# Stating the order of TensorE, ScalarE and VectorE in the units of two expert layers

## The chip, the core and the metric

One core of one Trainium2 chip runs the whole program in one launch. The metric is device time in microseconds (us) of that core; of the kernel before three runs are shown, and one more execution was profiled. Engines are named as in the profile: TensorE (PE, with its weight loads as PEld), VectorE (DVE), ScalarE (ACT), GpSimd (POOL) and SyncE (SP), which issues the loads of weights.

## The reference

Attention with pooled queries feeds two layers of experts, each of which sends a token to one expert. Cut to what matters:

```python
attn_out = softmax(scale * pool2(q) @ k.T) @ v          # 4 batches, 8 heads -> x of 2304 rows, 512 wide
# layer 1: only rows with x @ w_skip > 0, the others pass through
e = argmax(xc @ w_gate); g = softmax(xc @ w_gate)[e]
x[do_compute] = xc + g * (relu(xc @ w1[e]) @ w2[e])
# layer 2: all rows, with its own gate and an output gate
e = argmax(x @ w_gate2); g = softmax(x @ w_gate2)[e]; o = sigmoid(x @ w_output_gate)[e]
out = g * o * (relu(x @ w1b[e]) @ w2b[e])               # 8 experts a layer, 512 -> 1024 -> 512
```

## The kernel before, in words

**Attention** fills the first 575 us and is not touched by the change. At its end each token has been put into a table of its layer and expert, and from there the work goes in **units**: a unit takes up to 128 or 256 rows of one expert through both products. `unit(m, kind, e, pos)` (L964) emits one, with m = 0 for layer 1 and m = 1 for layer 2:

- P: 256 rows of an expert that was chosen early; it starts a layer and is emitted in the same block as the first F.
- F: the first 128 rows of every expert (up to 128, possibly none). It always runs.
- D: 256 more rows, in an `If` per number of rows that there are.
- S: a last 128 rows, in another `If`.

The loop at L1100 to L1116 emits for every expert F, then `If(code > 0)` (L1108) with up to eight nested `If`s that hold a D each (L1109) and one that holds S (L1114). In this data layer 1 runs P, F0, F1, F2 with two D, F3, F4, F5 with S, F6, F7; layer 2 runs P, F0, F1 with D, F2 with D, F3, F4 with D, F5 with three D, F6, F7 with S, as the stretches of TensorE's instructions show.

**Rows.** `fetch` (L822) reads the unit's place in the table and issues two indirect DMAs on POOL, each gathering 128 rows into xg. `xprep` (L211) turns them: TensorE transposes 128 columns at a time into pX (L215), ScalarE copies pX to xh as fp32r (L218), and VectorE takes the rest, xl (L219). A unit prepares the rows of the *next* unit; it fetches them near its own start.

**First product of F and S.** `gemm1_S` (L829) has rows as weights: two halves f of 512 columns, each 12 matmuls (L842), hooks between them, and a copy by ScalarE of each finished half (L846, into ht and xc). Then both halves are transposed (L851), and `relu_split` (L222) makes h: one ScalarE operation in layer 1 (L224), ScalarE and VectorE in layer 2 (hh at L227, hl at L228). D and P have weights as weights (`gemm1_D`, L231 to L241).

**Second product.** `gemm2` (L854) accumulates a row block into pY, in two halves f: in layer 1 four fp32 matmuls each (L860), in layer 2 twelve of fp32r each (L866). `evac` (L870 to L874) writes pY into yo on VectorE and `scatter` (L876) sends yo by an indirect DMA. The last `evac` of a unit is emitted as the first thing of the next one, behind a tiny POOL copy of indices (idp, L973).

**Weights of the next expert.** Of an expert's 16 chunks `split` (L190) casts one to fp32r on ScalarE (L205) and subtracts on VectorE to get the low half (L207); for layer 2 chunks 5, 7, 9, 11, 13 and 15 are subtracted on POOL. In layer 1 only chunks 0 to 7 are split. `pre` (L1005) does it for a list of chunks, in F and P alone. `load_w` and `load_w2` issue the loads on SP.

**Routing for layer 2.** Units of layer 1 route the rows they have just made: `route2` (L892) in four steps. Step 0 transposes yo and copies it (L889, L890), step 1 is a small product and a copy (L900, L901), step 2 a product (L914) and a chain of VectorE steps with two exponentials on ScalarE between (L916 to L929), step 3 a few tiny products and a last chain of VectorE steps (L933 to L953). `record` (L954) then writes two table rows by indirect DMAs on POOL.

**What sets the order.** Each engine runs its instructions in the order of the compiled program. In the units a scheduler chooses that order: it may bring an instruction forward past others that are not ready, and it may draw work past an `If`. Only edges made by `behind` hold something back. `foretell` (L1085) emits a branch hint for all engines: it loads the number of units from `mt` (a register load, L1103), computes a condition and issues the hint (L1150 in the profile). In F it is called by `ahead`, emitted after `load_w`.

In F and S of layer 1 `xprep` is held behind the first half of the second product (`XA = (1, 0)`); in layer 2 it is not.

Of the kernel before, what the change touches and what calls it, by code (L numbers as in the profile page):

```python
# [25 lines left out]
F = 1024  # L26
P = 128
# [31 lines left out]
JD = 8  # L59
POOL_L2 = (5, 7, 9, 11, 13, 15)  # L60
PS = (0, 1, 2, 4)
HP = (((1, 0, 1), (2, 2, 3), (3, 4, 5), (4, 6, 7)),) * 2
HR = ((1, 2, 2),) * 2
XA = (1, 0)
PB = (14, 16)
DVE_F = ((), ())
R2D = (2, 4, 5)
# [47 lines left out]
def build(ctx, tc, kT, qT, vt, wg, wa1, wa2, cst, out):  # L115
# [66 lines left out]
    def behind(i, js):  # L182
        for j in js:
            if j.ins.engine == i.ins.engine:
                tc.add_manual_dep(i.ins, j.ins.name,
                                  mybir.DependencyInfo(mybir.DependencyClass.NoSync, mybir.DependencyReason.DATA),
                                  reason="issue order")
        return i
# [22 lines left out]
    def xprep(n=2, after=()):  # L211
        o = []
        for h in range(n):
            for k in range(4):
                behind(nc.tensor.transpose(pX[h][:, k * P:(k + 1) * P], xg[:, h, k * P:(k + 1) * P], ident), after)  # L215
            px = pX[h].rearrange("p (k c) -> p k c", c=P)
            hs_ = slice(h * P, (h + 1) * P)
            o.append(nc.scalar.copy(xh[:, :, hs_], px))  # L218
            o.append(nc.vector.tensor_tensor(xl[:, :, hs_], px, xh[:, :, hs_].bitcast(F32), ALU.subtract))  # L219
        return o  # L220
# [30 lines left out]
    with ExitStack() as es_:  # L251
# [47 lines left out]
        pre = ap.tile([P, 96], F32, name="pre")  # L299
# [555 lines left out]
    def gemm2(m, i, o, h, fs):  # L855
        hc = slice(h * P, (h + 1) * P)
        for f in fs:
            if m == 0:
                for k in range(4):
                    j = nc.tensor.matmul(pY[o], hr[f][:, k, hc], w2r[i][:, 4 * f + k, :],  # L860
                                         start=(f + k == 0), stop=(f * k == 3))
                continue
            n = 12 * f
            for a, w in ((hh[f], w2h[i]), (hh[f], w2l[i]), (hl[f], w2h[i])):
                for k in range(4):
                    j = nc.tensor.matmul(pY[o], a[:, k, hc], w[:, 4 * f + k, :], start=(n == 0), stop=(n == 23))  # L866
                    n += 1
        return j

    def evac(m, h, tok):  # L870
        wv = tok[:, h, 1:2].bitcast(F32)
        if m == 0:
            return nc.vector.scalar_tensor_tensor(yo[:, h, :], pY[h], wv, xc[:, h, :], ALU.mult, ALU.add)
        return nc.vector.tensor_scalar(yo[:, h, :], pY[h], wv, None, ALU.mult)  # L874

    def scatter(m, h, tok, after=()):  # L876
        nc.gpsimd.tensor_copy(ids[h].bitcast(F32), tok[:, h, 0:1].bitcast(F32))
        i = nc.gpsimd.indirect_dma_start(  # L878
            out=(xb if m == 0 else out)[:, :],
            out_offset=bass.IndirectOffsetOnAxis(ap=ids[h].bitcast(U32), axis=0), in_=yo[:, h, :], in_offset=None,  # L880
            bounds_check=N - 1, oob_is_err=False)
        behind(i, after)
        for q in scat2[m] + (gath if m == 0 else []):
            tc.declare_no_dep(i.ins, q.ins, reason="every token has a row of its own")
        scat2[m].append(i)
# [69 lines left out]
    def record(h, after=()):  # L955
        i = nc.gpsimd.indirect_dma_start(
            out=tab[:, :], out_offset=bass.IndirectOffsetOnAxis(ap=pid2[:, h:h + 1], axis=0), in_=rec2[:, h, :],
            in_offset=None, bounds_check=2 * PC * P - 1, oob_is_err=False)
        behind(i, after)
        for q in scat:  # L960
            tc.declare_no_dep(i.ins, q.ins, reason="every token has a row of its own")
        scat.append(i)

    def unit(m, kind, e, pos, urgent=(), ahead=None):  # L964
        s = 9 * m + 1 + e
        i = s % 2
        first = kind == "P" and m == 0
        small = kind in "FS"
        pm = 0 if kind == "P" else m
        cp_ = nc.gpsimd.tensor_copy  # L970
        urgent = list(urgent)
        if not first:
            cp_(idp.bitcast(F32), idc.bitcast(F32))  # L973
            urgent.append(evac(pm, 1, idp))
        src = ts0 if first else idn
        if small:
            cp_(idc[:, 1, :].bitcast(F32), src[:, 0, :].bitcast(F32))
            nc.gpsimd.memset(idc[:, 0, 0:1], 1 << 20)
        else:
            cp_(idc.bitcast(F32), src.bitcast(F32))  # L980

        def head():
            if m == 0:
                if small:
                    nc.scalar.copy(xc[:, 1, :], xg[:, 0, :])
                else:
                    nc.scalar.copy(xc, xg)
            log = pm == 0 and not first and not (kind == "F" and e == 0)
            if log:
                record(0)  # L990
            g = fetch(m, pos) if kind != "P" else ()
            if not first:
                scatter(pm, 1, idp, g)
            if log:
                record(1, g)

        def r2(step):
            if pm == 0 and not first:
                route2(step)

        def pre(*cs):
            if kind in "FP":
                for c in cs:
                    split(s + 1, c, DVE_F[m], urgent if e == 0 else ())

        def half():
            evac(m, 0, idc)
            scatter(m, 0, idc)

        if kind == "D":  # L1010
            steps = {0: head, R2D[0]: lambda: r2(0), R2D[1]: lambda: r2(1), R2D[2]: lambda: r2(2)}
            gemm1_D(m, i, lambda c: steps[c]() if c in steps else None)
            gemm2(m, i, 0, 0, (0, 1))
            half()
            r2(3)
            xprep()
            gemm2(m, i, 1, 1, (0,))
            if m == 0:
                turn(0)
            if ahead:  # L1020
                ahead()
            gemm2(m, i, 1, 1, (1,))
            return
        if kind == "P":

            def post(c):
                if c == 0 and not first:
                    head()
                for r in range(4):
                    if PS[r] == c:  # L1030
                        r2(r)
                if c == 7:
                    if m:
                        record(0)
                        record(1)
                    unit_list(m)
                    nc.gpsimd.dma_start(ts[:, :PC, :], tabv[:, PC * m:PC * (m + 1), :])
                    fetch(m, 80, 1)
                if not first:
                    pre(c)  # L1040
                else:
                    for d in range(8):
                        if NP0 + d * (8 - NP0) // 8 == c:
                            pre(d)

            if first:
                head()
                load_w2(1)
            gemm1_D(m, i, post, range(NP0 if first else 0, 8))
            pre(*range(8, PB[m]))  # L1050
            gemm2(m, i, 0, 0, (0, 1))
            half()
            pre(*range(PB[m], 16))
            load_w(s + 2)
            gemm2(m, i, 1, 1, (0,))
            if m == 0:
                turn(0)
            j = gemm2(m, i, 1, 1, (1,))
            return xprep(1, after=[j])
        def hook(n):  # L1060
            if n == 0:
                head()
                if kind == "F" and m == 0:
                    load_w2(s + 1)
            for c in HP[m]:
                if c[0] == n:
                    pre(*c[1:])
            for c in range(3):
                if HR[m][c] == n:
                    r2(c)  # L1070

        gemm1_S(m, i, hook)
        j = gemm2(m, i, 1, 0, (0,))
        r2(3)
        xprep(2, [j] if XA[m] else ())
        pre(*range(8, 16))
        if kind == "F":
            load_w(s + 2)
            ahead()
        gemm2(m, i, 1, 0, (1,))  # L1080

    scat2 = [[], []]
# [5 lines left out]
    for m in range(2):  # L1088
# [7 lines left out]
        for e in range(E):  # L1096

            def ahead():
                if e == 0:
                    if m == 0:  # L1100
                        r = nc.gpsimd.value_load(eP[0:1, 3:4], min_val=0, max_val=7 * SL)
                        nc.gpsimd.dma_start(ts[:, PC:, :], tabv[:, PC:, :][:, ds(r, 2), :])
                    codes.extend(nc.values_load(mt[m][0:1, c:c + 1], min_val=0, max_val=18) for c in range(E))  # L1103
                foretell(f"any{m}{e}", codes[e] > 0)
# [49 lines left out]
```

## Time and profile before

| what | us |
|---|---|
| three runs | 1168.31, 1170.78, 1175.32 (median 1170.78) |
| the profiled execution, its own time | 1175.5 |
| span in the profile | 1173.8 |
| PE / DVE / ACT / POOL busy | 1056.1 / 764.5 / 567.9 / 362.2 |

The profile covers one execution; times in its rows count from the first instruction. The groups of instructions name what is written and read (out<-in), how often, the busy time, the mean duration in ns, and after the bar the idle time of that engine just before them with what ended it. A timeline row gives the start, the duration and, in brackets, the idle time before it. PEclk is the share of full speed that TensorE's clock was granted; it has two levels, 1.2 and 2.4 GHz.

### The profile page before, as it was taken

How to read it: one execution, taken by the hardware profiler on the slowest of the kernel's cores; microseconds unless marked ns; L12 is line 12 of the kernel's file. 1: busy time of each engine (PE TensorE's matmuls, PEld its weight loads, DVE VectorE, ACT ScalarE, POOL GpSimd, SP SyncE). 2: the span in 40 equal slices, each digit the busy share in tenths (PEclk: the TensorE clock that was granted, in tenths of full speed). 3: DMA queues.
4: the chain of work that ended last, by engine and by line, in shares of the span. 5: the costliest groups of instructions: out<-in, count | busy, mean ns of one | idle time of the engine just before them, and what ended most of it. 6: DMA issues, size and time to landing. Idle time of an engine off the chain costs nothing. (4 is left out here: it accounts for less than half of the span.)

```text
span 1173.8 us, 19240 instructions
## 1 busy us (share of the span) xinstructions
PE 1056.1 (90%) x6400; PEld 762.3 (65%) x6400; DVE 764.5 (65%) x1423; ACT 567.9 (48%) x1395; POOL 362.2 (31%) x429
## 2 busy tenths in 40 slices
PE   4799998999989999899998999998869887899977
PEld 2566665666656666675755765565758676788865
DVE  6789998899899998976355224546664437262252
ACT  3566665566656666555355224545363435231141
POOL 6222222212242221210224123344563526151151
PEclk9799998999999999999999999999999898999989
DMA  9644442244444431137277205854574527251010
GB/s 230 160 115 114 107 111 62 71 112 101 112 102 112 106 93 37 40 96 240 65 241 255 92 28 193 256 166 156 178 233 134 172 65 254 67 190 36 30 40 18
DMA packets 72946, 146.47 MB, mean 125 GB/s; under 512 B 12652, under 2 KB 21612, under 8 KB 72738
## 3 DMA queue, kind: packets, MB, share of 16 engines
q1 hardware_dynamic: 63330, 127.65, 37.6%
q0 software_dynamic: 9408, 16.48, 4.6%
q8 instruction: 77, 1.26, 0.5%
q14 instruction: 131, 1.07, 0.3%
HBM read 138.18 MB, written 15.05 MB: 131 GB/s over the span
## 5 line engine op out<-in xcount | busy, mean ns | idle before, releaser
L409 ACT ACTIVATE PT<-pS 128x288 f32<-128x288 f32 x576 | 206.5, 409 | 148.4 <-PE pS L408 145.2
L382 DVE TENSOR_REDUCE mx<-pA 128x1 f32<-128x1152 f32 x144 | 194.9, 1356 | 32.5 <-PE pA L377 20.3
L405 PE MATMUL pS<-QQ,KK 128*128 128x288 f32 x576 | 185.6, 335 | 22.2 <-ACT PT L409 21.1
L416 PE MATMUL pO<-PT,V 128*64 128x288 f32 x1152 | 181.0, 425 | 0.0
L408 PE MATMUL pS<-QM,KB 73*128 73x288 f32 x576 | 167.2, 302 | 0.0
L405 PEld LDWEIGHTS pS<-QQ,KK 128*128 128x128 f32 x576 | 111.3, 193 | 74.8 <-ACT PT L409 31.7
L362 POOL TENSOR_TENSOR QM<-qs,QQ 64x576 fp32r<-64x576 f32 x32 | 48.3, 1512 | 320.5 <-ACT QQ L348 248.8
L408 PEld LDWEIGHTS pS<-QM,KB 73*128 73x128 f32 x576 | 112.2, 195 | 0.0
L377 PE MATMUL pA<-KK,QQ 128*128 128x384 f32 x384 | 94.5, 357 | 18.4 <-DVE KK L332 10.0
L416 PEld LDWEIGHTS pO<-PT,V 128*64 128x64 f32 x1152 | 72.6, 137 | 55.1 <-issue 26.6
L860 PE MATMUL pY<-w2r,hr 128*128 128x512 f32 x240 | 108.1, 596 | 0.4 <-issue 0.4
L205 ACT CAST w1h<-raw 128x512 fp32r<-128x512 f32 x141 | 78.9, 621 | 51.5 <-PEq L1114 27.0
L429 DVE TENSOR_TENSOR acc<-acc,PT 128x576 f32<-128x576 f32 x128 | 95.1, 762 | 4.4 <-ACT PT L409 3.4
L207 DVE TENSOR_TENSOR w1l<-raw,w1h 128x512 fp32r<-128x512 f32 x126 | 88.7, 743 | 12.3 <-ACT w1h L205 11.2
L218 ACT CAST xh<-pX 128x512 fp32r<-128x512 f32 x56 | 30.9, 589 | 128.5 <-PE pX L215 101.8
L237 PE MATMUL pH<-xh,w1h 128*128 128x256 f32 x312 | 90.8, 291 | 1.3 <-DVE hl L228 1.0
L237 PE MATMUL pH<-xl,w1h 128*128 128x256 f32 x312 | 88.8, 285 | 1.2 <-DVE xl L219 1.2
L237 PE MATMUL pH<-xh,w1l 128*128 128x256 f32 x312 | 88.4, 284 | 0.0
L842 PE MATMUL pH<-w1h,xh 128*128 128x512 f32 x144 | 62.1, 431 | 22.6 <-ACT w1h L205 13.9
L377 PEld LDWEIGHTS pA<-KK,QQ 128*128 128x128 f32 x384 | 67.3, 200 | 22.3 <-DVE mx L382 11.7
L228 DVE SCALAR_TENSOR_TENSOR hl<-pH,hh 128x256 fp32r<-128x256 f32 (+1 forms) x74 | 36.0, 486 | 61.3 <-ACT hh L227 58.5
L860 PEld LDWEIGHTS pY<-w2r,hr 128*128 128x128 f32 x240 | 43.5, 190 | 46.0 <-issue 42.5
(219 smaller groups left out, 1969.3 us busy)
## 6 DMA issues: line engine op xcount, KB each, us to landing
raw<-wa SPq DMA_DIRECT2D x216, 256.0 KB
rawQ<-qT SPq DMA_DIRECT2D x64, 288.0 KB
rawK<-kT SPq DMA_DIRECT2D x64, 288.0 KB
w2r<-wa SPq DMA_DIRECT2D x72, 256.0 KB
V<-vt SPq DMA_DIRECT2D x16, 576.0 KB
xb<-xr SPq DMA_DIRECT2D x14, 288.0 KB
xg<-xb,idn POOLq DMA_INDIRECT x54
xb<-xr POOLq DMA_DIRECT2D x2, 288.0 KB
```

The costliest lines, as they stand in the source:

```text
L205: behind(nc.scalar.copy(h, r), after)
L207: behind(eng.tensor_tensor(l, r, h.bitcast(F32), ALU.subtract), after)
L237: nc.tensor.matmul(o, w[:, k, cc], x[:, k, :], start=(n == 0), stop=(n == 11))
L377: nc.tensor.matmul(o, QQ[h][i][:, u * P:(u + 1) * P], KK[h][i][:, cc], start=True, stop=True)
L382: i = nc.vector.tensor_reduce(mx[p % 2 if p or t < 5 else 1][:, t:t + 1], pA[:, :, :384], AX.XY, ALU.max)
L405: m = nc.tensor.matmul(o, KK[h][i][:, k], QQ[h][i][:, c], start=True, stop=False)
L408: nc.tensor.matmul(o, KB[h][p % 2][:64 + NB, k], QM[h][i][:64 + NB, c], start=False, stop=True)
L409: exps.append(nc.scalar.activation(PT[(p * KT + j) % 4][h][:, c], o, AF.Exp, scale=0.0625))
L416: i = nc.tensor.matmul(pO[f][64 * h:64 * h + 64, :HQ], V[p % 3][:, j, h, :], PT[(p * KT + j) % 4][h][:, c], start=(j == 0), stop=(j == KT ...
L429: nc.vector.tensor_tensor(a, a, t, ALU.add)
L842: nc.tensor.matmul(pH[f], x[:, k, :P], w[:, k, fc], start=(n == 0), stop=(n == 11))
L860: j = nc.tensor.matmul(pY[o], hr[f][:, k, hc], w2r[i][:, 4 * f + k, :], start=(f + k == 0), stop=(f * k == 3))
```

## The change

Four things. (1) Units F, D and S are emitted inside a region in which TensorE, ScalarE and VectorE issue their instructions in the order of the source; POOL and SP stay the scheduler's, and so does P. (2) In F and S the order of the source itself changes: chunks 6 and 7 are split after both transposed halves instead of after the first product's second half, step 2 of `route2` comes one hook later, and `xprep` stands behind the first half of the second product in both layers, between chunks 8 to 11 and 12 to 15. (3) `ahead`, the hint, follows `xprep` in F; in D of layer 1 it goes before the transposes of `turn`. (4) On POOL the first `record` also goes behind the two gathers.

```diff
-HP = (((1, 0, 1), (2, 2, 3), (3, 4, 5), (4, 6, 7)),) * 2
-HR = ((1, 2, 2),) * 2
-XA = (1, 0)
+HP = ((1, 0, 1), (2, 2, 3), (3, 4, 5), (6, 6, 7))
+HR = (1, 2, 3)
...
-    def unit(m, kind, e, pos, urgent=(), ahead=None):
+    def unit(m, kind, *a):
+        if kind == "P":
+            return unit_(m, kind, *a)
+        ET = mybir.EngineType
+        with tc.manual_schedule(engines={ET.PE, ET.Activation, ET.DVE}):
+            return unit_(m, kind, *a)
+
+    def unit_(m, kind, e, pos, urgent=(), ahead=None):
...
-            if log:
-                record(0)
             g = fetch(m, pos) if kind != "P" else ()
             if not first:
                 scatter(pm, 1, idp, g)
             if log:
+                record(0, g)
                 record(1, g)
...
             gemm2(m, i, 1, 1, (0,))
+            if ahead:
+                ahead()
             if m == 0:
                 turn(0)
-            if ahead:
-                ahead()
             gemm2(m, i, 1, 1, (1,))
...
-            for c in HP[m]:
+            for c in HP:
                 if c[0] == n:
                     pre(*c[1:])
             for c in range(3):
-                if HR[m][c] == n:
+                if HR[c] == n:
                     r2(c)
 
         gemm1_S(m, i, hook)
-        j = gemm2(m, i, 1, 0, (0,))
+        gemm2(m, i, 1, 0, (0,))
         r2(3)
-        xprep(2, [j] if XA[m] else ())
-        pre(*range(8, 16))
+        pre(*range(8, 12))
+        xprep(2)
+        if kind == "F":
+            ahead()
+        pre(*range(12, 16))
         if kind == "F":
             load_w(s + 2)
-            ahead()
         gemm2(m, i, 1, 0, (1,))
```

## Rows read from the trace of the kernel before

**Rows 1.** Layers 1 and 2: PE, PEld, DVE, ACT, POOL busy (x), PEclk, DMA share, GB/s.

```profile
575.00:820.00 245.00, 230.40 (x1131) 146.12 (x1129) 115.05 (x406) 106.29 (x223) 88.08 (x125) 1.00 0.52 166
820.00:1174.00 354.00, 302.49 (x1658) 256.77 (x1657) 161.43 (x243) 125.98 (x255) 144.27 (x189) 0.95 0.37 119
```

**Rows 2.** Groups of PE instructions in layer 2 (820 to 1174 us).

```profile
L866 PE MATMUL pY<-w2h,hl 128*128 128x512 f32 x184 | 52.5, 408 | 8.7 <-DVE hl L228 8.7
...
L842 PE MATMUL pH<-w1h,xh 128*128 128x512 f32 x72 | 30.8, 428 | 15.6 <-ACT w1h L205 9.6 <-ACTq L1108 3.1 <-DVEq L1109 1.3
...
L215 PE MATMUL pX<-cs,xg 128*128 128x128 f32 x124 | 19.5, 291 | 14.9 <-DMA xg<-xb,idn 14.9
```

**Rows 3.** Groups of PE instructions in layer 1 (575 to 820 us).

```profile
L215 PE MATMUL pX<-cs,xg 128*128 128x128 f32 x92 | 12.4, 277 | 2.5 <-DMA xg<-xb,idn 2.5
L889 PE MATMUL pX<-cs,yo 128*128 128x128 f32 x56 | 8.9, 279 | 2.3 <-DVE yo L873 2.2
```

**Rows 4.** Timeline of PE in F1 of layer 2, from its transposes on.

```profile
875.47 0.60 PE L851 MATMUL pH<-cs,ht 128*128 128x128 f32 x4
880.70 0.80 PE L215 MATMUL pX<-cs,xg 128*128 128x128 f32 x4 [4.64 <-DMA xg<-xb,idn]
881.30 1.06 PE L851 MATMUL pH<-cs,xc 128*128 128x128 f32 x4
...
886.36 1.18 PE L866 MATMUL pY<-w2h,hh 128*128 128x512 f32 x4
...
888.30 0.86 PE L866 MATMUL pY<-w2h,hl 128*128 128x512 f32 x3
```

**Rows 5.** Timeline of DVE in F4 of layer 2.

```profile
984.53 7.33 DVE L207 TENSOR_TENSOR w2l<-raw,w2h 128x512 fp32r<-128x512 f32 x1 [0.35 <-DMA raw<-wa]
```

**Rows 6.** Timeline of POOL in the same unit.

```profile
985.11 2.53 POOL L207 TENSOR_TENSOR w1l<-raw,w1h 128x512 fp32r<-128x512 f32 x2
987.60 3.71 POOL L207 TENSOR_TENSOR w2l<-raw,w2h 128x512 fp32r<-128x512 f32 x3
```

**Rows 7.** The same columns in two stretches that follow an idle TensorE.

```profile
914.80:917.80 3.00, 2.96 (x8) 2.37 (x9) 0.00 (x0) 2.16 (x5) 0.00 (x0) 0.57 0.03 8
...
712.00:715.00 3.00, 2.79 (x14) 2.24 (x15) 2.10 (x5) 1.80 (x4) 1.68 (x6) 1.00 0.83 258
```

**Rows 8.** Timeline of PE: first matmul of F2 in layer 2, of F3 in layer 1.

```profile
914.85 0.47 PE L842 MATMUL pH<-w1h,xh 128*128 128x512 f32 x1 [2.02 <-ACT w1h L205]
...
712.21 0.49 PE L842 MATMUL pH<-w1h,xh 128*128 128x512 f32 x1 [1.82 <-ACT w1h L205]
```

**Rows 9.** Timeline of ACT in F4 of layer 1.

```profile
729.26 1.14 ACT L205 CAST w1h<-raw 128x512 fp32r<-128x512 f32 x2 [2.89 <-PEq L1108]
731.36 0.62 ACT L985 COPY xc<-xg 128x512 f32<-128x512 f32 x1 [0.96 <-DVE yo L873]
...
737.50 0.58 ACT L846 COPY xc<-pH 128x512 f32<-128x512 f32 x1
...
739.32 0.20 ACT L928 ACTIVATE s<-s 128x2 f32<-128x2 f32 x1
```

**Rows 10.** Timeline of DVE in the same unit.

```profile
730.57 0.75 DVE L873 SCALAR_TENSOR_TENSOR yo<-pY,idp,xc 128x512 f32<-128x512 f32 x1 [3.17 <-ACT w1h L205]
...
738.75 0.17 DVE L927 TENSOR_REDUCE s<-sm 128x2 f32<-128x16 f32 x1
...
745.23 0.67 DVE L219 TENSOR_TENSOR xl<-pX,xh 128x512 fp32r<-128x512 f32 x1
```

**Rows 11.** Timeline of PE in the same unit.

```profile
729.93 0.49 PE L842 MATMUL pH<-w1h,xh 128*128 128x512 f32 x1 [0.80 <-ACT w1h L205]
...
738.66 3.68 PE L860 MATMUL pY<-w2r,hr 128*128 128x512 f32 x8
```

**Rows 12.** PE's branch past an expert's D and S: after F0 and F4 of layer 1.

```profile
L1108 PEldq COMPARE_BRANCH  x1: 4680/4680/4680, 611.2 to 611.2; - x1
...
L1108 PEldq COMPARE_BRANCH  x1: 353/353/353, 743.3 to 743.3; - x1
```

## The prediction, made before the changed kernel ran

> **What bounds the kernel now.** I read the two layers as stretches first. TensorE works 230.4 of 245 us in layer 1 and 302.5 of 354 us in layer 2 [rows 1], so it sets the pace, and what can be won is its idle time and its clock. The clock is granted in full in layer 1, but only 0.95 of it in layer 2: 0.05 x 354 = 17.7 us lost. Then the groups of TensorE instructions, for what ended its idle time. In layer 2: 14.9 us before the transposes of gathered rows (L215), 8.7 us before the matmuls that read hl, 15.6 us at the first matmul of an F or S [rows 2]. In layer 1 the transposes wait only 2.5 us for rows and 2.3 us for yo [rows 3].
>
> The timeline shows why. In F1 of layer 2 the scheduler has put the transposes of xg *between* the two groups of L851: TensorE finishes four transposes at 876.1 and stands until the rows land at 880.70, with all of the second product still to do [rows 4]. In F4 VectorE sits 7.33 us in one subtraction [rows 5], while POOL runs five subtractions from 985.11 to 991.31 [rows 6], and hl is queued behind it. After such idle times the clock falls: PEclk 0.57 in the 3 us after the 2.02 us gap before F2, against 1.00 after 1.82 us of idle at F3 of layer 1 [rows 7, 8]. Layer 2 has ten such falls, P and the tail included, so about 1.7 us each.
>
> **Layer 2, part by part.**
>
> 1. *Rows transposed later.* The transposes now come after the other four transposes (0.60 us) and half a product (3.0 us, like the 12 matmuls from 886.36 on): TensorE asks for the rows 3.6 us later in the unit. The wait of 4.64 us [rows 4], the longest, would leave 1.0. But POOL is not ordered and does not begin earlier when TensorE ends its unit earlier, so part of what is won comes back as wait in the next unit. I leave 6 of the 14.9 us [rows 2]: -8.9. Bounds: 0 (all comes back) and -14.9.
> 2. *hl ahead of the subtractions.* In the source hl is emitted before chunks 8 to 15, and chunks 6 and 7 now stand behind it too: the 8.7 us [rows 2] go. -8.7.
> 3. *xl behind them instead.* VectorE must now finish chunks 8 and 10 before xl, and a subtraction that meets a run of POOL's has taken 7.33 us [rows 5]. xl is not needed until the next unit's third matmul, which 3.0 us of matmuls cover; one that is caught so makes TensorE wait up to 7.33 - 0.68 - 3.0 = 3.6 us. Seven F units: 0 to +25. Chunks come later now and POOL has gaps between them, so nearer the lower end: +4.
>    The Trainium skill (SBUF — State Buffer, Who interferes with whom) says that a VectorE operation with two SBUF inputs and a GpSimd operation that reads SBUF exclude each other for one instruction. By that a wait would be at most one POOL subtraction, which the matmuls cover, so the term would be 0 and the sum 1154, inside the forecast's own range. The row shows a wait for five in a row, so I keep +4.
> 4. *The hint leaves the unit's start.* A register load, a condition and the hint stood before the first matmul of a unit, an estimated 0.6 of the 0.80 us idle there [rows 11]. Where F follows D (F2, F3, F5, F6) that is won: -2.4. Where F follows F, the hint now comes just before the branch; F0 of layer 1 already had it there, and its branch took 4.68 us against 0.35 with the hint at the start [rows 12]. Half a product and the eight transposes cover 3.9 of it, the rest eats the 0.6. Bounds -4.2 and +1.
> 5. *The clock.* Each fall comes behind one of the long waits named so far; items 1, 2 and 4 take most of these away. Of 17.7 us, P and the tail keep 3.5; the falls at F5, whose unit start is not shortened enough, and behind a wait in F1 or F2 stay. I take -8. Bounds 0 and -14.
>
> Layer 2: -8.9 - 8.7 + 4 - 2.4 - 8 = **-24**, between about -14 and -36.
>
> **Layer 1.** Here `xprep` already stood behind the first half, so the order of the others decides. I walk through F4, counted from its first matmul at 729.93 [rows 11]. VectorE writes yo by +1.4 [rows 10]. ScalarE today runs two casts ahead of xc [rows 9]; stated, xc is first (it waits for yo), then casts 0 and 1, x2T, ht, casts 2 and 3, lg2, casts 4 and 5: ten steps, each adding 0.52 us (two casts take 1.14, one operation alone 0.62 [rows 9]), to about +6.6. VectorE subtracts chunk 5 by +7.4 and only then takes the routing chain: nine dependent steps of 0.17 us [rows 10], 0.2 with the handover, to +9.2. Now the point: both exponentials of that chain are emitted *before* ScalarE's copy of the second half. Today the copy starts at 737.50, between the two, and the second exponential stands at 739.32, behind both relus [rows 9]. Stated, the copy waits for the second exponential (0.20), ends at +10.0, and the second product starts at +10.6 instead of +8.7 (738.66) [rows 11]. TensorE idles 2.0 us of it, between the two groups of transposes: +1.9 a unit. Queued behind the waiting copy on ScalarE are both relus and casts 6 and 7; TensorE waits for copy and relu, nobody yet for the casts.
>
> The hint gives 0.6 back at the start. VectorE's tail (13 steps of routing, then xl) ends later than today's 745.90 [rows 10], while the next unit begins with its write of yo: 0 to +1.4, I take 0.6, near the middle, since no row shows it. So +1.9 a unit; for F1 to F7 +13.3 (bounds 0 and +20). The waits for yo of today (2.3 us, mostly F7, where VectorE ran chunks for layer 2) go by 1.8. `record` behind both gathers lets these issue earlier on POOL by one indirect DMA, enough with the later request to end the waits of 2.5 us; the record itself has no reader before layer 2. SP's loads keep their place. The 2.0 us of idle are as long as the 2.02 after which the clock fell, but layer 1 kept it after 1.82 [rows 7, 8]: 0 to 8 falls of 1.7 us, I take one or two, +2.5, as today it has none.
>
> Layer 1: 13.3 - 1.8 - 2.5 + 2.5 = **+11.5**, between -4 and +26. D in both layers is full of matmuls and its order hardly changes: 0, covered by 12 matmuls a chunk.
>
> **Sum.** -24 + 11.5 = -12.5. The profiled execution took 1175.5, which becomes 1163; it stood 4.7 above the median of 1170.8, so the forecast is **1158 us**. About 0.5%, 5.9 us, is what a measurement of this kernel can tell from no change.
>
> **Rivals.**
>
> - *Slower: the exponentials decide.* Place: ScalarE's copy of the second half in each F and S of layer 1. If the idle 2.0 us lowers the clock every time (1.7) and VectorE is late at each next start (1.4), a unit costs 4.5, eight of them 36, less 4.3 for the waits that go: +32 against -24. 1170.8 + 8 = 1179. It decides from 3.5 us a unit on. For it: the chain is forced by the emitted order. Against: today's clock in layer 1 is 1.00 throughout [rows 1].
> - *No change: POOL's subtractions catch xl.* By 3.6 us at the four F with a D behind, 14.4 instead of 4: -2 in all, 1169. For it: the 7.33 us [rows 5]. Against: POOL gets its chunks in smaller runs.
> - *Far faster: layer 1 costs nothing.* If VectorE takes the routing chain early enough, layer 1 gives -4.3 (the waits that go), and if no row is waited for in layer 2 and xl is covered, layer 2 gives -14.9 - 8.7 - 2.4 - 8 = -34: 1170.8 - 38 = 1133. For it: all 14.9 us are waits for transfers that other work can cover [rows 2]. Against: both conditions must hold, and the emitted order speaks against the first.
> - *The change doesn't reach what matters:* POOL's order stays free, and if POOL gathers later, part 1 gives 0 and half of the clock stays lost: about 1171, counted with no change.
>
> **How the numbers follow.** Forecast 0.50, slower 0.20, no change 0.20, far faster 0.10. The forecast's own range is 1146 to 1168, so a tenth of it lies within 0.5%: faster 0.45 + 0.10 = 0.55, same 0.25, slower 0.20. The range, 1141 to 1179, takes in the two middle rivals and the bounds; it leaves out the tails.
>
> **What would show it.** Right: L215 in layer 2 waits 6 us instead of 14.9; no wait for hl; PEclk of layer 2 at 0.97 or above; in layer 1 a wait of about 2 us for ScalarE before the second L851 of every F. Wrong: no such wait in layer 1 (the step on the exponentials fails), waits for xl above 4 us (part 3), PEclk below 0.97 in layer 1 (the slower rival), or gathers that land as late relative to the request as before (part 1).

## The result and the profile after

The changed kernel takes 1185.54 us (median of 20 runs, 1174.25 to 1197.87), the kernel before 1168.31 (20 runs beside them, 1161.74 to 1179.80): ratio 1.0118, 95% interval 1.0089 to 1.0147. The ratio is taken over the fast runs alone (18 of the changed kernel's 20) and is not that of the two medians, which is 1.0147. The changed kernel is slower; the forecast was 1158, and the measured time lies above the range. The profiled execution took 1186.02 us with a span of 1184.3, 10.5 more than that of before.

I divide both traces at the same three places, the first matmul of F0 of layer 1, of P of layer 2, and of F0 of layer 2, and end at the last second product. Windows, the kernel before; after the stretch come its length, the busy times of PE, PEld, DVE, ACT and POOL, then PEclk, the DMA share and GB/s:

```profile
599.10:820.35 221.25, 207.12 (x1016) 131.30 (x1014) 104.04 (x363) 96.95 (x203) 77.20 (x111) 1.00 0.53 169
820.35:852.40 32.05, 27.09 (x169) 23.59 (x169) 21.16 (x55) 12.90 (x30) 17.16 (x24) 0.95 0.57 182
852.40:1166.70 314.30, 275.23 (x1488) 233.18 (x1488) 139.52 (x187) 113.08 (x226) 126.11 (x164) 0.95 0.35 114
```

The same of the changed kernel:

```profile
597.20:830.30 233.10, 210.91 (x1015) 131.10 (x1015) 102.59 (x358) 96.39 (x203) 74.92 (x113) 0.99 0.50 159
830.30:868.35 38.05, 30.06 (x169) 26.88 (x170) 24.29 (x64) 13.07 (x30) 19.38 (x26) 0.82 0.53 167
868.35:1177.10 308.75, 274.33 (x1488) 231.09 (x1488) 150.17 (x187) 113.61 (x226) 128.69 (x164) 0.96 0.36 117
```

Layer 1 lost 11.9 us, P of layer 2 another 6.0, layer 2's units won 5.6, and F0 began 1.9 earlier: +10.5. Forecast for these were +11.5, 0 and -24. So the question is layer 2, and P. In layer 2 TensorE idles 39.1 us of the stretch before (length less PE busy) and 34.4 after.

**Layer 2.** Groups of PE instructions of the changed kernel from F0 of layer 2 to the end; they answer to [rows 2]:

```profile
L236 PE MATMUL pH<-xl,w1h 128*128 128x256 f32 x192 | 55.1, 287 | 3.5 <-DVE xl L218 3.5
...
L865 PE MATMUL pY<-w2h,hl 128*128 128x512 f32 x168 | 47.3, 404 | 0.8 <-DVE hl L227 0.8
...
L841 PE MATMUL pH<-w1h,xh 128*128 128x512 f32 x72 | 31.1, 432 | 17.8 <-DVEq L1115 8.5 <-PEq L1121 4.1 <-ACT w1h L204 2.9
...
L214 PE MATMUL pX<-cs,xg 128*128 128x128 f32 x120 | 17.1, 279 | 10.1 <-DMA xg<-xb,idn 10.1
L850 PE MATMUL pH<-cs,xc 128*128 128x128 f32 x36 | 5.9, 286 | 2.6 <-ACT xc L845 2.6
```

The wait for hl is gone (8.7, now 0.8). But rows still cost 10.1 us, the unit starts 17.8 instead of 15.6, now mostly behind VectorE (DVEq is its sequencer, here at a branch), xl 3.5, and ScalarE's copy of the second half 2.6. Where VectorE was, DVE and then POOL in F4:

```profile
1002.15 7.34 DVE L206 TENSOR_TENSOR w1l<-raw,w1h 128x512 fp32r<-128x512 f32 x1
1009.41 1.28 DVE L206 TENSOR_TENSOR w2l<-raw,w2h 128x512 fp32r<-128x512 f32 x2
1010.62 1.27 DVE L218 TENSOR_TENSOR xl<-pX,xh 128x512 fp32r<-128x512 f32 x2
```

```profile
997.02 1.52 POOL L825 DMA_INDIRECT xg<-xb,idn  x1 [0.73 <-PE pH L841]
998.57 1.29 POOL L206 TENSOR_TENSOR w2l<-raw,w2h 128x512 fp32r<-128x512 f32 x1
1000.02 1.30 POOL L825 DMA_INDIRECT xg<-xb,idn  x1 [0.16 <-issue]
1001.62 1.03 POOL L877 DMA_INDIRECT out<-yo,ids  x1 [0.30 <-DVE hl L227]
1002.69 2.51 POOL L206 TENSOR_TENSOR w1l<-raw,w1h 128x512 fp32r<-128x512 f32 x2
1005.15 3.78 POOL L206 TENSOR_TENSOR w2l<-raw,w2h 128x512 fp32r<-128x512 f32 x3
```

One subtraction, 0.68 us long elsewhere, stands for as long as POOL does five, as in [rows 5, 6]. hl now passed before it; xl, behind it, makes the D after F4 wait 3.5 us. The same rows bear on the gathered rows, too: POOL, whose order is free, runs a subtraction between the two gathers of F4 and begins them 3.0 us apart. It does so in F2 to F6, and in F2, F3, F4 and F6 TensorE waits 3.45, 3.75, 0.94 and 1.55 us before its second four transposes, 9.7 of the 10.1. In the kernel before, the two began 1.4 to 1.9 us apart in these units, so that 1.1 to 1.6 us of each wait can come from this. And ScalarE in F2:

```profile
939.63 0.58 ACT L217 CAST xh<-pX 128x512 fp32r<-128x512 f32 x1 [0.69 <-ACT w2h L204]
944.20 0.58 ACT L217 CAST xh<-pX 128x512 fp32r<-128x512 f32 x1 [3.98 <-PE pX L214]
944.68 2.18 ACT L204 CAST w2h<-raw 128x512 fp32r<-128x512 f32 x4
```

In the stated order the casts of chunks 12 to 15 stand behind the copies of the gathered rows. Here the second half's rows land at 943.00, so the casts begin at 944.68.

**Layer 1.** PE in F4, then ScalarE in the same unit; they answer to [rows 11] and [rows 9]:

```profile
743.34 0.60 PE L850 MATMUL pH<-cs,ht 128*128 128x128 f32 x4
745.70 0.66 PE L850 MATMUL pH<-cs,xc 128*128 128x128 f32 x4 [1.76 <-ACT xc L845]
```

```profile
743.68 0.22 ACT L924 ACTIVATE sm<-sm 128x16 f32<-128x16 f32 x1 [1.41 <-DVE sm L918]
744.97 0.20 ACT L927 ACTIVATE s<-s 128x2 f32<-128x2 f32 x1 [1.07 <-DVE s L926]
745.08 0.57 ACT L845 COPY xc<-pH 128x512 f32<-128x512 f32 x1
```

This is the step of the forecast, seen as it was worked out: the copy stands behind both exponentials, and TensorE idles 1.76 us between the transposes. In the groups of layer 1, the kernel before and then the changed one:

```profile
L851 PE MATMUL pH<-cs,xc 128*128 128x128 f32 x36 | 5.9, 287 | 1.9 <-issue 1.2 <-ACT xc L846 0.5
```

```profile
L859 PE MATMUL pY<-w2r,hr 128*128 128x512 f32 x208 | 95.9, 606 | 2.2 <-issue 2.2
...
L850 PE MATMUL pH<-cs,xc 128*128 128x128 f32 x36 | 5.9, 286 | 14.5 <-ACT xc L845 14.5
```

**P of layer 2** has a new wait of 4.1 us at its second matmul, the first that reads xl, and the lower of the two clock levels, 1.2 GHz, over more of its length (PEclk 0.82 on the mean, before 0.95). TensorE idles 8.0 us in P, 3.0 more than before, and is busy 3.0 longer. PE, then VectorE:

```profile
830.34 0.36 PE L236 MATMUL pH<-xh,w1h 128*128 128x256 f32 x1 [0.15 <-PEq L1115]
834.77 0.58 PE L236 MATMUL pH<-xl,w1h 128*128 128x256 f32 x1 [4.08 <-DVEq L1115]
```

```profile
832.38 1.28 DVE L218 TENSOR_TENSOR xl<-pX,xh 128x512 fp32r<-128x512 f32 x2
833.58 0.68 DVE L206 TENSOR_TENSOR w2l<-raw,w2h 128x512 fp32r<-128x512 f32 x1
834.89 0.71 DVE L206 TENSOR_TENSOR w2l<-raw,w2h 128x512 fp32r<-128x512 f32 x1 [0.63 <-DVEq L1115]
```

xl is written at 833.66, but the wait lasts until VectorE has finished one more subtraction and passed its branch out of F7 (L1115), just before 834.77. So P waits for VectorE's work in F7, not for xl alone.

### The profile page after: what moved, and what is told of

Its sections match the earlier page's. It is cut to its first block, busy times and chain, and to the rows that moved or that the text cites. A ratio compares the mean times of both kernels' runs of the same rounds, so it can differ in the third digit from the quotient of the medians.

```text
span 1184.3 us, 19280 instructions
## 1 busy us (share of the span) xinstructions
PE 1061.2 (90%) x6400; PEld 762.4 (64%) x6400; DVE 777.1 (66%) x1423; ACT 567.8 (48%) x1395; POOL 363.8 (31%) x429
## 5 line engine op out<-in xcount | busy, mean ns | idle before, releaser
L206 DVE TENSOR_TENSOR w1l<-raw,w1h 128x512 fp32r<-128x512 f32 x126 | 111.9, 928 | 47.8 <-ACT w1h L204 47.4
L376 PE MATMUL pA<-KK,QQ 128*128 128x384 f32 x384 | 94.6, 357 | 18.6 <-DVE KK L331 9.9
L236 PE MATMUL pH<-xl,w1h 128*128 128x256 f32 x312 | 91.2, 292 | 7.6 <-DVEq L1115 4.1
L841 PE MATMUL pH<-w1h,xh 128*128 128x512 f32 x144 | 63.1, 438 | 21.4 <-DVEq L1115 8.5
L376 PEld LDWEIGHTS pA<-KK,QQ 128*128 128x128 f32 x384 | 67.1, 199 | 23.0 <-DVE mx L381 12.6
```

What stands on the lines that cost most here:

```text
L206: behind(eng.tensor_tensor(l, r, h.bitcast(F32), ALU.subtract), after)
L236: nc.tensor.matmul(o, w[:, k, cc], x[:, k, :], start=(n == 0), stop=(n == 11))
L376: nc.tensor.matmul(o, QQ[h][i][:, u * P:(u + 1) * P], KK[h][i][:, cc], start=True, stop=True)
L841: nc.tensor.matmul(pH[f], x[:, k, :P], w[:, k, fc], start=(n == 0), stop=(n == 11))
```

## Experiments

Ratios are to runs of the kernel before on the same chip, with the 95% interval. The three stretches are the lengths between the marks above; before 221.3, 32.1, 314.3, changed kernel 233.1, 38.1, 308.8. They come from one execution each, and times of one kernel differ by up to 1.5% (1161.7 to 1179.8 before).

**1. Stated order in one layer alone.**

```diff
-        if kind == "P":
+        if kind == "P" or m == 0:      # second run: m == 1
             return unit_(m, kind, *a)
```

> Only layer 2 keeps the stated order; the units of layer 1 are ordered by the scheduler again, with the rest of the change in place. Theory (the trace compared stretch by stretch): layer 1 gives back its 12 us (the waits of about 1.8 us for ScalarE before the second half's transposes go), P of layer 2 its 6 us (VectorE no longer comes into P with work of F7 still to do), and layer 2 keeps its gain of 5 to 6: about 1165, or 0.993 to 0.998 of the kernel before. Rival (not the stated order but the source's other edits, the hint and the record, cost the time): layer 1 stays as long as after the change, and the kernel at 1180 or above.

> Only layer 1 keeps the stated order; the units of layer 2 are ordered by the scheduler. Theory: layer 1 is 12 us and P of layer 2 is 6 us longer than before, and layer 2's F0 to the end goes back to about the 314 us of the kernel before: 1186 or more, a little slower than the whole change. Rival (the stated order of layer 2 is worth nothing, and the source's new order of gathers, record and hint gave the 5.5 us there): as the whole change, F0 to the end at 309.

Layer 2 alone: 1.0160 (1.0118 to 1.0202). P is back at 30.4 and layer 2 at 306.2, but layer 1 takes 242.7, still longer: left to the scheduler, the new source order makes TensorE wait 15.6 us for gathered rows there, where it was 2.5 [rows 3]. The theory fell for layer 1: without the stated order the new source does more harm there. Among its edits is the loss of `XA`, which had held `xprep` behind the first half of the second product; in this trace two of the eight transposes of xg stand between the two groups of L850, as in [rows 4], with a wait of 5.82 us in F0. That this edit alone does it was not run. Layer 1 alone: 1.0126 (1.0086 to 1.0165); the stretches are 233.5, 37.5 and 313.2. The theory holds for layer 1 and P: 12 and 5 us appear with the stated order in layer 1 alone. That the stated order wins the 5.6 us of layer 2 is not shown: the time, 1180.9 where 1186 was expected, is no longer than the changed kernel's (1.0118), and the profiled execution was the slowest of six. TensorE idles 33.2 us in its layer 2, no more than the changed kernel's 34.4; the difference is busy time at a lower clock (280.0 against 274.3, PEclk 0.93 against 0.96).

**2. The exponentials behind the copy.**

```diff
-            nc.scalar.activation(ex, d, AF.Exp)         # and exp(-z), step 2
+            if not late: ...                            # late: F and S
...
+        if late:                                        # start of step 3
+            nc.scalar.activation(ex, d, AF.Exp)
+            nc.scalar.activation(z, z, AF.Exp, scale=-1.0)
```

> The changed kernel, but in F and S both exponentials of the routing stand behind ScalarE's copy of the second half and the relus instead of ahead of them. Theory (the exponentials hold the copy back): the eight waits of about 1.8 us before the second half's transposes shrink to under 0.3 each, layer 1 is 12 us shorter, and the kernel 1171 to 1174. Rival (ScalarE or VectorE is the real limit of these units, and the wait only moves to the unit's end or to the next unit's xl): the waits go, but others of more than 1 us a unit appear, and the kernel stays above 1179.

1172.26, ratio 1.0043 (1.0016 to 1.0070): some 9 us better than the changed kernel's 1.0118. Stretches 225.5, 38.1, 311.0. PE's group in layer 1 of this run:

```profile
L850 PE MATMUL pH<-cs,xc 128*128 128x128 f32 x36 | 5.9, 286 | 2.1 <-ACT xc L845 2.1
```

14.5 became 2.1, and layer 1 is 7.6 shorter in this trace, in which the clock fell in F0 and S. The exponentials are the largest single loss of layer 1. P keeps its 38.

**3. Hint at the unit's start; one code load a unit.**

```diff
+                if kind == "F" and e:          # run 1: hook(0); gone from behind xprep for e > 0
+                    ahead()
...
-   codes.extend(nc.values_load(mt[m][0:1, c:c + 1], ...) for c in range(E))    # run 2
+   codes.append(nc.values_load(mt[m][0:1, e:e + 1], ...))                      # for every e
```

> The changed kernel with the branch hint of F1 to F7 at the unit's start. Theory (the long starts of layer 2 wait for VectorE's last subtractions, which stand behind ScalarE's casts, and the hint costs no more than 0.6 us where F follows F): within 3 us of the changed kernel; the 4.1 us before F7 of layer 2 stay above 3. Rival (the late hint makes the branch slow, and that is what the starts of F1, F5 and F7 wait for): the start of F7 falls below 1.5 us, and the kernel gains 5 us or more.

> The changed kernel, but each F loads its own branch code alone where F0 loaded all eight on every engine. Theory (in the stated order the eight loads of F0, about 0.3 us each, stand in TensorE's and ScalarE's queues ahead of the second half's products and of the casts of chunks 12 to 15): the 2.2 us of idle in F0 of layer 1 fall below 0.8, the 4.35 us before F1 of layer 2 below 2.5, and the kernel is 3 to 5 us faster than the changed one. Rival (the loads are hidden, and the branch's own fetch of code makes the gaps): both gaps stay within 0.5 us, no gain.

Hint at the start: 1.0186 (1.0132 to 1.0241). The stretches are 241.4, 38.2 and 309.1, so layer 2 is as before this edit: the late hint is not what its starts wait for. Layer 1 is 8 us longer in this trace, because the clock fell in F2 to F5 and in F7, to 0.91 or 0.92 on the mean where the changed kernel has 1.00: TensorE is busy 7.0 us longer. Two of the six runs, 1180.2 and 1181.9, are as fast as the changed kernel's, and the intervals of the ratios overlap, so that the hint's place brings these falls is not shown. One load: 1.0162 (1.0119 to 1.0205), no gain in time, although layer 2 is 302.7 in the trace. In F0 of layer 1 the gap between the transposes and the second half's products is gone (2.18 us, then none), as expected. The start of F1 in layer 2 only fell from 4.38 to 3.73, and 2.5 was expected: the loads were a small part of that wait.

**4. xl ahead of chunks 8 to 11.**

```diff
-        pre(*range(8, 12))
         xprep(2)
+        pre(*range(8, 12))
```

> The changed kernel with the gathered rows' xh and xl ahead of chunks 8 to 11 (in layer 1 only F7 has such chunks). Theory (xl behind the subtractions is what P of layer 2 and the D behind F4 wait for): the wait for xl of 4.1 us in P falls below 1.2 and the one of 3.5 us behind F4 below 1; TensorE's clock in P falls once less. Price: the casts of chunks 8 to 11 stand behind ScalarE's copies of the rows too, so where rows are late (F2, F3) the next units' starts get later by up to 2 us. Sum: 3 to 8 us faster than the changed kernel. Rival (VectorE is behind by all it has to do in F7, whatever its order): P's wait stays above 3 us in another place, no gain.

1.0137 (1.0103 to 1.0170), not told apart from the changed kernel. The wait behind F4 is gone, but four waits for hl of 1.3 to 3.0 us stand in F2, F3, F4 and F6, and the start of F1 waits 6.6. Rows cost nothing in layer 2 (10.1 us in the changed kernel), and its stretch is 300.3, yet the kernel is not faster. In P the wait is still 3.0, although xl is written by 831.19 there: three subtractions of F7 behind it run until 834.43, and the wait ends with VectorE's branch, as above. The waits change places; the rival is right about P.

**5. No subtraction on POOL, in the changed kernel.**

```diff
-POOL_L2 = (5, 7, 9, 11, 13, 15)
+POOL_L2 = ()
```

> The changed kernel with all subtractions of layer 2's chunks on VectorE, none on POOL. Theory (a VectorE subtraction that meets a run of POOL's waits until the run ends: 7.34 us from 1002.15 on, while POOL did five): no subtraction of VectorE in layer 2 takes over 2.5 us, the 3.5 us wait for xl behind F4 goes, and the gathers land earlier. Against that VectorE has six more subtractions of 0.68, 4 us, in each F of 15 to 19 us: 0 to 6 us faster than the changed kernel. Rival (VectorE becomes the bound of layer 2's F): waits for VectorE at the unit starts grow by 2 us or more each, slower by 5 or more.

1.0019 (0.9991 to 1.0047): about 12 us better than the changed kernel, where 0 to 6 were expected. Layer 2's window of this run, then its two groups of VectorE subtractions:

```profile
867.50:1159.90 292.40, 269.79 (x1488) 228.11 (x1488) 135.07 (x229) 113.60 (x226) 77.08 (x122) 0.97 0.38 123
```

```profile
L206 DVE TENSOR_TENSOR w2l<-raw,w2h 128x512 fp32r<-128x512 f32 x56 | 35.4, 686 | 10.7 <-DVEq L1121 5.8 <-ACTq L1121 2.6 <-ACT w2h L204 2.2
L206 DVE TENSOR_TENSOR w1l<-raw,w1h 128x512 fp32r<-128x512 f32 x56 | 35.2, 685 | 13.5 <-ACT w1h L204 13.5
```

With 42 instructions more, VectorE is busy *less*: 135.1 us against 150.2. The same groups of the kernel before, from F0 of layer 2 to the end, and of the changed kernel:

```profile
L207 DVE TENSOR_TENSOR w2l<-raw,w2h 128x512 fp32r<-128x512 f32 x28 | 44.4, 1615 | 2.2 <-ACT w2h L205 1.5 <-DMA raw<-wa 0.3 <-issue 0.3
L207 DVE TENSOR_TENSOR w1l<-raw,w1h 128x512 fp32r<-128x512 f32 x42 | 29.8, 772 | 3.4 <-ACT w1h L205 3.4
```

```profile
L206 DVE TENSOR_TENSOR w1l<-raw,w1h 128x512 fp32r<-128x512 f32 x42 | 56.0, 1379 | 6.8 <-ACT w1h L204 6.5
...
L206 DVE TENSOR_TENSOR w2l<-raw,w2h 128x512 fp32r<-128x512 f32 x28 | 29.9, 1107 | 2.1 <-ACT w2h L204 2.1
```

Above 0.685 us a piece the 70 subtractions lose 28 x 0.93 + 42 x 0.09 = 30 us before and 42 x 0.69 + 28 x 0.42 = 41 after the change: the change made VectorE meet POOL more, not less. It is not the stated order that does so: with layer 2 left to the scheduler (experiment 1, layer 1 alone; means of 1805 and 864 ns) the same sum is 39 us.

**6. Parts together.** The first run joins three of the edits above, the second adds the POOL edit, the third also this:

```diff
+        if kind == "F" and m == 0 and e == 6:     # and F7 leaves them out
+            for c in range(8, 15):
+                split(s + 2, c)
```

> Three parts at once on the changed kernel: exponentials behind the second half's copy, one code load a unit, and in layer 1 the gathered rows ahead of chunks 8 to 11. Theory (the three losses are separate): 9 to 12 us from the first, 3 to 5 from the second, 3 to 6 in P from the third: 1163 to 1169, level with the kernel before or better. Rival (the losses hide one another): no better than the exponentials alone, 1172 or above.

> The three parts together (exponentials behind the copy, one code load a unit, layer 1's rows ahead of chunks 8 to 11) and no subtraction of layer 2 on POOL. Theory (the losses of layer 1 and the lock between POOL and VectorE in layer 2 are separate): layer 1 as in the run of the three (220 us from F0 to P, 233 in the changed kernel), layer 2 from F0 to the end as in the run without POOL (292 us, 309 in the changed kernel), P 36 to 39: 1153 to 1158. Rival (both runs won from the same source): no better than 1166.

> As the kernel of the four parts, and besides chunks 8 to 14 of the weights for layer 2's P are written in F6 of layer 1 and not in F7. Theory (before the change the scheduler ran seven of them between 792 and 801, in F6; the stated order keeps all sixteen in F7, and P begins with VectorE behind): P falls from 36 to 39 us to 32 to 34, F7 stays within 1 us, so 3 to 5 us faster than the four parts. Rival (F6 has no room on VectorE either): F6 or the start of F7 gets longer by what P wins.

The three parts: 1.0038 (1.0016 to 1.0059), 1172.4, no better than the exponentials alone: the rival, though the trace's layer 1 is down to 220.1. With POOL's subtractions gone: 0.9922 (0.9891 to 0.9953), 1161.4, between the theory and its rival; layer 2 took 291.3 as expected, layer 1 225.7 where 220 was expected. Chunks in F6: 0.9927 (0.9897 to 0.9956), no gain. P falls from 36.6 to 32.3, and F7 grows from 19.6 to 22.5. So 4.3 of P's 6 us hang on these seven of F7's sixteen chunks. Half of F7's growth is a lower clock (0.92; TensorE busy 18.6 us, without this edit 17.1), so the rival, that there is no room for them, is not shown.

**7. POOL and the rows in the kernel before.** Edits of the kernel before, each alone or as named: POOL without subtractions, with three (5, 9, 13), rows later (`XA = (1, 1)`), and both. One more run has layer 1 as before, and layer 2 as changed without POOL's subtractions.

> The kernel before, with no subtraction of layer 2 on POOL and nothing else. Theory (the lock between POOL and VectorE costs the kernel before as well, and the change's gain in layer 2 is mostly this): the two waits for hl of over 4 us go, gathers land earlier: F0 to the end 314 becomes 298 to 304, 0.987 to 0.992 of the kernel before. Rival (without a stated order VectorE's six more subtractions stand ahead of hl and xl): waits for hl and at unit starts grow, no gain or slower, and only the stated order makes use of the idle POOL.

> Layer 1 with the order and the source of the kernel before (also its records, hints and eight code loads), layer 2's units in the stated order as changed, and no subtraction of layer 2 on POOL. Theory (layer 1 and P lose 18 us by the change alone, and layer 2 gains 16 us without POOL): F0 to P 221, P 32, layer 2 292: 1147 to 1153, 0.982 to 0.987. Rival (the first run, in which layer 1 alone was left to the scheduler and took longer, not shorter): F0 and F7 of layer 1 again 7 us longer each, 1165 or more.

> The kernel before with one thing changed: in layer 2 too the gathered rows are transposed between the halves of the second product; the scheduler still orders everything. Theory (half a product, 3.0 us, is put between the request and the row's landing, and part of it comes back since POOL does not begin earlier): the wait of 14.2 us before the transposes falls to 6 to 10, but xl is then written later and meets POOL's runs: 0.993 to 1.002 of the kernel before. Rival (the later rows are worth their whole 8.9 us, and it was the stated order that lost them): 0.990 or less.

> The kernel before without POOL's subtractions, and the rows between the halves in layer 2. Theory (with POOL free the gathers land earlier, and the waits left before the transposes are 5.5 us): at most 3 us of them go: 0.981 to 0.987, level with the run without POOL alone at 0.985. Rival (xl, later by half a product, makes the next unit wait for VectorE, which has all subtractions): 0.988 or more.

> The kernel before with three subtractions a unit on POOL (chunks 5, 9 and 13) where it has six. Theory (a VectorE subtraction waits for the end of the run of POOL's it meets, so shorter and fewer runs cost less): the longest subtraction of VectorE in layer 2 falls from 7.4 to 4 us or less, the time lost in them from 30 us to 8 to 15, and the kernel stands between the two, 0.989 to 0.996. Rival (any work of POOL's in the way is enough, since the gathers wait for it too): level with the kernel before, 0.998 or more.

| kernel | us | ratio (95%) | layer 2, F0 to the end | of it TensorE idle |
|---|---|---|---|---|
| before | | 1 | 314.3 | 39.1 |
| before, no POOL | 1153.2 | 0.9846 (0.9807 to 0.9885) | 290.2 | 19.8 |
| layer 1 as before, layer 2 stated, no POOL | 1156.1 | 0.9886 (0.9846 to 0.9925) | 299.7 | 27.1 |
| before, rows later | 1182.9 | 1.0108 (1.0064 to 1.0153) | 321.3 | 38.8 |
| before, rows later, no POOL | **1144.8** | 0.9802 (0.9757 to 0.9848) | 286.8 | 19.0 |
| before, half of POOL | 1159.2 | 0.9915 (0.9877 to 0.9953) | 297.3 | 24.2 |

Without POOL's subtractions the kernel before beats what the theory expected of it: layer 2 takes 290.2, where 298 to 304 were expected and 314.3 was before. Its waits for hl and for rows:

```profile
L866 PE MATMUL pY<-w2h,hl 128*128 128x512 f32 x168 | 45.9, 395 | 0.0
...
L215 PE MATMUL pX<-cs,xg 128*128 128x128 f32 x122 | 17.9, 278 | 5.5 <-DMA xg<-xb,idn 5.5
```

Of the 24 us, 8.7 are the wait for hl, and as many are waits for rows (14.2, now 5.5), which POOL itself gathers. In F1 POOL began its first gather 4.1 us after the unit's first matmul, and begins it 1.5 us after it here. So POOL's subtractions cost time in two ways, by holding VectorE and by making POOL late with the gathers. Taking them away ends both at once, and no run separates the two. The remainder is 1.2 us of waits for xl, 0.8 at the unit starts and 4.8 of TensorE's busy time, with PEclk at 0.97.

The stated order adds nothing to that: 1156.1 beside 1153.2, where 1147 to 1153 was expected, and layer 2 at 291.3, 292.4, 293.3 and 299.7 in the four traces that have both.

The rows alone do the opposite of what I forecast. PE groups of layer 2 in that run:

```profile
L866 PE MATMUL pY<-w2h,hl 128*128 128x512 f32 x168 | 50.2, 423 | 20.6 <-DVE hl L228 20.5
...
L215 PE MATMUL pX<-cs,xg 128*128 128x128 f32 x120 | 18.4, 302 | 0.9 <-DMA xg<-xb,idn 0.9
```

The wait for rows is almost gone, 0.9, and the wait for hl has grown to 20.5 from 8.7. VectorE and POOL in F0 of layer 2 there:

```profile
859.66 8.70 DVE L207 TENSOR_TENSOR w2l<-raw,w2h 128x512 fp32r<-128x512 f32 x2 [0.83 <-DMA raw<-wa]
868.28 0.68 DVE L228 SCALAR_TENSOR_TENSOR hl<-pH,hh 128x512 fp32r<-128x512 f32 x1
```

```profile
859.77 2.53 POOL L207 TENSOR_TENSOR w1l<-raw,w1h 128x512 fp32r<-128x512 f32 x2
862.24 4.96 POOL L207 TENSOR_TENSOR w2l<-raw,w2h 128x512 fp32r<-128x512 f32 x4
```

In part the wait for rows had covered VectorE's; besides, VectorE is now held longer, 47 us above 0.685 a piece (means of 2121 and 845 ns) where it was 30. TensorE idles as long as before, 38.8 us: the waits have only changed places. The 7 us that layer 2 lost are busy time at a lower clock (282.5 against 275.2, PEclk 0.93 against 0.95). With POOL's subtractions gone the same edit shows no wait for hl, 2.0 us for rows, and the shortest time of all, 0.9802, so it beats both kernels. The 1.1% that the later rows cost alone is gone. That they gain is not shown: beside POOL's removal alone (0.9846) the intervals overlap, and TensorE's idle time is 19.0 against 19.8.

With half of POOL's subtractions about half is lost. VectorE's subtractions in that run:

```profile
L207 DVE TENSOR_TENSOR w2l<-raw,w2h 128x512 fp32r<-128x512 f32 x42 | 39.8, 981 | 0.3 <-ACT w2h L205 0.3
L207 DVE TENSOR_TENSOR w1l<-raw,w1h 128x512 fp32r<-128x512 f32 x49 | 33.4, 744 | 4.9 <-ACT w1h L205 4.9
```

Lost above 0.685: 42 x 0.30 + 49 x 0.06 = 15 us, half of the 30, and the time stands halfway. The longest subtraction took 3.55 us, and rows cost 8.0 us, again about halfway.

## Why the prediction was wrong

- **Layer 1, the exponentials (+13.3):** the mechanism was right. ScalarE's copy costs 14.5 - 1.9 = 12.6 us more, about 1.8 in seven of the nine F and S of layer 1, and moving the two instructions gave some 9 us back. The waits for yo (now 0.2) and rows (now none) went as forecast. The sum, 11.9 against 11.5, is nearer than its terms, which is luck: the unit starts of F1 to F7 fell by 2.8 us (7.4 to 4.6), which the forecast had cancelled against a late VectorE; F0 lost 2.2 to eight code loads, which I had not counted as the stated order's; and TensorE was busy 3.8 us longer, with one fall of the clock in F1 (0.92), where 2.5 was put for one or two.
- **P, counted at nothing:** the first step that failed. P has no stated order, but F7 has. Before, the scheduler had drawn seven of P's chunks out of F7 into F6 (casts from 792 to 799). I read the late yo of F7 from it, counted 1.8 us of gain, and did not ask where the chunks would go. In F7's own order they keep VectorE in F7 past the start of P, and P lost 6.0, half of it idle and half at the lower clock.
- **Layer 2, -24 forecast and -5.6 measured:** the step that decided is that the waits of items 1 and 2 and the clock of item 5 were priced each as its own and taken off one by one. Measured by the waits from F0 on: rows 14.2 to 10.1 and hl 8.7 to 0.8, so 12 us in place of 17.6; against that the unit starts +2.2 (item 4 had -2.4), xl +2.3 (item 3 had +4) and the copy +2.5 (not counted), so -5.0 in all. The waits shared a source, POOL's subtractions (without them hl costs nothing and rows 5.5): they hold VectorE 30 us, late for whatever stands next in its order, and they make POOL late with the gathers. The run with rows later alone shows it plainest: 14.2 + 8.7 = 22.9 us of waits before, 0.9 + 20.5 = 21.4 after.
- **Item 5, the clock (-8):** the largest single miss. PEclk went from 0.95 to 0.96, and PE's busy time fell by 0.9 us only. TensorE's idle time had fallen by 4.7 us only, in other places.
- **Item 3** named the mechanism, and "POOL's subtractions catch xl" was a rival. It was priced at four places and only for xl; in the traces it holds hl, xl, the subtractions themselves and with them the next unit's start. The row of 7.33 us [rows 5] was the thing to follow: the mean of the w2l group, 1615 ns, was in the trace of before, beside single ones of 0.68 us.
- **The slower rival** gave 1179 with the exponentials as its place. Its direction came true, by another sum: layer 1 as forecast, P besides, and a layer 2 that won 5.6 instead of 24.
- **The range** was narrower than its terms: the bounds of items 1 to 5 add up to -42 and +17, and layer 2 was given -36 to -14. The measured -5.6 lies outside the second and inside the first.

## What to carry to other kernels

Before taking a wait off the path, ask whether the engine that ends it is late in general: then the wait moves to its next reader, and only its cause is worth removing. Compare one instruction's mean duration across a stretch with its shortest; a mean of 1.6 us over 0.68 is a contention to price as a whole. Divide a stretch into TensorE's idle and busy time before naming what an edit won: here a wait that went often came back in another place, and part of the time went with the clock. When an order is fixed by hand, list what the scheduler had moved across branches, since that work comes back into the unit that owns it.

## What was not expected of the hardware

A VectorE subtraction of two operands in SBUF that meets POOL subtractions issued back to back can be held until their run ends, not for one of them: 7.34 us in F4 over five that take 6.3 together, while POOL's kept their length (1.26 each, one alone 1.29). It had begun 0.5 us before the first of them, but POOL was then in an indirect DMA, from 1001.62 to 1002.65. In the kernel before, too, POOL had an indirect DMA or a subtraction under way when each of the four that took over 4 us began. In layer 2 no subtraction was over 0.72 us once POOL had none. It is not always so. In F0 of the changed kernel, VectorE and POOL (second view) take turns, and both are held:

```profile
877.96 3.14 DVE L206 TENSOR_TENSOR w2l<-raw,w2h 128x512 fp32r<-128x512 f32 x2 [0.26 <-ACT w2h L204]
```

```profile
877.48 1.37 POOL L206 TENSOR_TENSOR w1l<-raw,w1h 128x512 fp32r<-128x512 f32 x1 [1.65 <-ACT w1h L204]
878.81 3.44 POOL L206 TENSOR_TENSOR w2l<-raw,w2h 128x512 fp32r<-128x512 f32 x2
```

The Trainium skill (SBUF — State Buffer, Who interferes with whom) has the lock last for one instruction, held by whoever issues first. The turns agree with that. In F4 VectorE did not get it between two of POOL's five, and there the measurement decides. What makes the one or the other happen was not tried.

With the hint at the start the clock fell to 1.2 GHz in part of F3, F4 and F5 of layer 1 (0.92 on the mean), where TensorE idled 1.80, 1.85 and 1.89 us between the transposes; in the changed kernel it idled 1.81, 1.76 and 1.80 there and stayed at 2.4 GHz (1.00). In F1 of the changed kernel the clock fell (0.92) with 1.79 us there. So the length of this gap alone does not tell. What separates them was not tried.
